# Dealing seven key tiles of two head pairs out around the sums and values of the preceding pairs in a fused attention and MLP kernel

## The chip, the cores and the metric

The kernel runs on one core of a Trainium2 chip. The metric is the device time of one execution in microseconds (us), the median over the runs shown. TensorE (PE) does the matrix products, ScalarE (ACT) the exponentials and activations, VectorE (DVE) reductions, scalings and copies, GpSimd (POOL) the squares and the loads that change type, and SyncE (SP) issues most other transfers. Each engine works through its own instructions strictly in the program's order.

## What is computed

Cosine attention over 8 batches of 12 heads, 448 positions of 64 numbers each, followed by a two-layer network with a leaky ReLU over all 3584 tokens.

```python
q_n = q / (np.linalg.norm(q, axis=-1, keepdims=True) + 1e-06)
k_n = k / (np.linalg.norm(k, axis=-1, keepdims=True) + 1e-06)
scores = np.matmul(q_n, k_n.transpose(0, 1, 3, 2)) / tau
scores = scores - np.max(scores, axis=-1, keepdims=True)
attn = np.exp(scores)
attn = attn / (np.sum(attn, axis=-1, keepdims=True) + 1e-09)
attn_out = np.matmul(attn, v)
...
x = np.ascontiguousarray(attn_out.transpose(0, 2, 1, 3)).reshape(B * S, H * D)
h = x @ w_in            # 768 -> 2048
g = np.maximum(0.01 * h, h)
return (g @ w_out).astype(np.float32)   # 2048 -> 768
```

## The kernel before

**Slots and pairs.** A slot `s` is two heads of one batch; there are 6 slots in a batch and 48 in all. Two consecutive slots, an even one and the odd one after it, make four heads. `j = s // 2 - 1` names the four heads whose sums and values are worked while the scores of slot `s` are made.

**Attention of a slot.** `load_qk(s)` (L94) issues four transfers on SP: queries, keys and two remainders of 64 rows. `squares(s)` (L130) squares them on POOL, `sums(s)` (L143) adds the squares up on DVE, `roots(s)` (L154) makes the norms with three small ACT instructions, and `normalise(s)` (L163) divides on DVE: one reciprocal and two multiplications into `qn`. `transposes(s)` (L194) turns `qn` into `qkT`. For slots under 10 this is seven PE transposes into PSUM and a DVE copy; from slot 10 on it is one transposing transfer on SP (`DMA_FROM = 10`).

**Key tiles.** The 448 keys of a head are three tiles of 128 and a rest of 64. `scores(s, kis)` (L210) issues for each tile `ki` the matmuls for both heads, then the exponentials on ACT. Tiles 0 to 2 use half of PE's rows for each head (64 rows by 128 columns), so both heads run side by side. Tile 3 holds the rests of both slots of a pair, so there are seven key tiles to two slots; it uses quarters of 64 by 64 and is made with the odd slot. The score pool `p_sc` has two buffers, so a key tile needs the exponential of the tile two before it.

**Sums and values.** `totals(j)` (L254) multiplies the exponentials by ones, `products(j, e)` (L264) by the even or odd columns of the values, both through `strip_products` (L242) in four column strips of 32 that run side by side: 16 matmuls each, 48 in all for one `j`. ACT makes the reciprocal sums (`rb`, L258 and L259), and `scale(j, e)` (L272) multiplies on DVE into `xT`.

**The network.** The tokens are cut into eight chunks of 384 or 512 columns in turn. `first(c, m)` (L287) makes one of 16 groups of 6 matmuls with an ACT activation into `hT`; `second(c, ts, half)` (L314) makes one of 6 or 8 groups of 16 matmuls with a DVE copy, and stores after the second half. All of these use the full 128 by 128 array. The list `work` (L343) gives each group a place, measured in slots: chunk `c` spreads over the six slots from `6(c+1)`. `feed(place)` (L358) issues all groups whose place has come. The PSUM pool `p_mm` has four buffers, shared by sums, values and groups.

**The order around the change.** The schedule is written out by hand. After an opening of six slots (L420), the main loop (L467) goes slot by slot. An even slot issues sums and values of the preceding four heads, key tiles 0 and 1, groups, the norms and transposes of slot `s + 2`, the loads of slot `s + 5`, key tile 2, groups. An odd slot does the same without sums and values, and ends with key tiles 2 and 3 together. On SP the transposing transfers, the loads and the stores stand in one queue in this order.

```python
for s in range(NPAIR, NSLOT + 1):
    j = s // 2 - 1 if s % 2 == 0 else None
    n = s + 2
```

Of the kernel before, what the change touches and what calls it, by code (L numbers as in the profile page):

```python
# [16 lines left out]
def kernel(  # L17
# [10 lines left out]
    nc = tc.nc  # L28
# [8 lines left out]
    NPAIR = H // 2  # L37
# [4 lines left out]
    HALF = D_model // 2  # L42
    DMA_FROM = 10
    WARM = 22
    assert REM == 64 and D == 64

    ctx.enter_context(tc.manual_schedule())
    cpool = ctx.enter_context(tc.tile_pool(name="consts", bufs=1))
    ldp = ctx.enter_context(tc.tile_pool(name="ld", bufs=4))
    vbp = ctx.enter_context(tc.tile_pool(name="vb", bufs=4))  # L50
    sqp = ctx.enter_context(tc.tile_pool(name="sq", bufs=2))
    smp = ctx.enter_context(tc.tile_pool(name="small", bufs=3))
    qnp = ctx.enter_context(tc.tile_pool(name="qn", bufs=3))
    qtp = ctx.enter_context(tc.tile_pool(name="qt", bufs=5))
# [58 lines left out]
    def load_v(j):  # L113
        if j >= B * NQ:
            return
        b, jj = divmod(j, NQ)
        vb[j] = vbp.tile([128, 4, 3, D], BF16, name="v_b")
        gp.dma_start(out=vb[j], in_=main(v, b, 4 * jj, 4))  # L118

    def load_v_rem(b):  # L120
        if b >= B:
            return
        r = v[b, :, MAIN:S].rearrange("(j g) p d -> g p j d", g=4)
        for g in range(4):
            lo = 64 * (g // 2)
            gp.dma_start(out=vrb[b % 2][lo : lo + 64, :, g], in_=r[g])  # L126
# [3 lines left out]
    def squares(s, engs=(gp, gp)):  # L130
        if s >= NSLOT:
            return
        tiles = []
        for x, eng, name in zip(raw[s], engs, ("sq0", "sq1")):
            sq = sqp.tile(list(x.shape), F32, name=name)
            if eng is nc.scalar:
                nc.scalar.activation(sq, x, func=AF.Square)  # L137
            else:
                eng.tensor_tensor(sq, x, x, op=ALU.mult)  # L139
            tiles.append(sq)  # L140
        sqs[s] = tiles
# [12 lines left out]
    def roots(s):  # L154
        if s >= NSLOT:
            return
        nc.scalar.activation(ss[s], ss[s], func=AF.Ln, bias=tiny)
        nc.scalar.activation(ss[s], ss[s], func=AF.Exp, scale=0.5)
        nc.scalar.activation(ss[s], ss[s], func=AF.Identity, bias=eps)  # L159
# [3 lines left out]
    def normalise(s):  # L163
        if s >= NSLOT:
            return
        r = smp.tile([128, 14], F32, name="r")
        nc.vector.reciprocal(r, ss[s])  # L167
        qn[s] = qnp.tile([128, 7, 2, D], BF16, name="qn")
        for x, lo, hi, r0 in ((raw[s][0], 0, 4, 0), (raw[s][1], 4, 7, 8)):
            nt = hi - lo  # L170
            nc.vector.tensor_tensor(  # L171
                qn[s][:, lo:hi],
                x.rearrange("p h t d -> p t h d"),
                r[:, r0 : r0 + 2 * nt].rearrange("p (h t) -> p t h", h=2)
                .unsqueeze(3).to_broadcast([128, nt, 2, D]),
                op=ALU.mult,
            )
# [32 lines left out]
    def scores(s, kis):  # L210

        if s >= NSLOT:
            return
        tiles = []
        for ki in kis:
            sc = scp.tile([128, 2, 512], F32, name="sc")
            tiles.append(sc)
            for i in range(2 if ki == 3 else 1):
                x = qkT[s - 1 + i] if ki == 3 else qkT[s]
                for a in range(2):  # L220
                    rows = slice(64 * a, 64 * a + 64)
                    out = sc[64 * i : 64 * i + 64] if ki == 3 else sc
                    c0, c1 = (448, 512) if ki == 3 else (512 + 128 * ki, 640 + 128 * ki)
                    nc.tensor.matmul(  # L224
                        out=out[:, a, :S], lhsT=x[rows, c0:c1], rhs=x[rows, 0:S],
                        start=True, stop=True,
                    )
        for ki, sc in zip(kis, tiles):
            if ki == 3:
                pr[s // 2] = prp.tile([128, 2, S], BF16, name="pr")  # L230
                dst = pr[s // 2]
            else:
                if s not in pe:
                    pe[s] = pep.tile([128, 3, 2, S], BF16, name="pe")
                dst = pe[s][:, ki]
            nc.scalar.activation(out=dst, in_=sc[:, :, :S], func=AF.Exp, scale=inv_tau)  # L236
# [17 lines left out]
    def totals(j):  # L254
        sm = mmp.tile([128, 512], F32, name="sm", tag="mm")
        strip_products(j, sm, lambda g, ki: ones, lambda g: ones_rem[:, g // 2])
        rb = rbp.tile([128, S], F32, name="rb")
        nc.scalar.activation(rb, sm[:, :S], func=AF.Ln)  # L258
        nc.scalar.activation(rb, rb, func=AF.Exp, scale=-1.0)  # L259
        rbs[j] = rb  # L260
# [3 lines left out]
    def products(j, e):  # L264
        b, jj = divmod(j, NQ)
        po = mmp.tile([128, 512], F32, name="po", tag="mm")
        pos[j, e] = po
        vm = vb[j].rearrange("p h t (d e) -> p h t e d", e=2)
        vr = vrb[b % 2].rearrange("p j g (d e) -> p j g e d", e=2)
        strip_products(j, po, lambda g, ki: vm[:, g, ki, e], lambda g: vr[:, jj, g, e])  # L270

    def scale(j, e):  # L272
        b, jj = divmod(j, NQ)
        m, half = divmod(b, 2)
        if m not in xT:
            xT[m] = xtp.tile([128, KT, 2 * S], BF16, name="xT")
        nc.vector.tensor_tensor(  # L277
            xT[m][:, 2 * jj + e, half * S : (half + 1) * S], pos.pop((j, e))[:, :S], rbs[j],
            op=ALU.mult,
        )  # L280
# [33 lines left out]
    def second(c, ts, half):  # L314
        c0, n = chunk_cols(c)
        po2 = mmp.tile([128, 512], F32, name="po2", tag="mm")
        for m in range(MT):
            nc.tensor.matmul(  # L318
                out=po2[:, :HALF],
                lhsT=hT[c][:, m, ts * 128 : (ts + 1) * 128],  # L320
                rhs=w_out_sb[:, m, half * HALF : (half + 1) * HALF],
                start=(m == 0), stop=(m == MT - 1),
            )
        if half == 0:
            osb[c, ts] = osp.tile([128, D_model], F32, name="osb")
        o = osb[c, ts]
        nc.vector.tensor_copy(out=o[:, half * HALF : (half + 1) * HALF], in_=po2[:, :HALF])  # L327
        last = c == B - 1 and ts == n // 128 - 1
        if half == 1 or last:
            h0 = half * HALF if last else 0  # L330
            x, end, row = c0 + ts * 128, c0 + (ts + 1) * 128, 0
            while x < end:
                dst, cnt = rows_of(c, x, end)
                nc.sync.dma_start(
                    out=dst[:, h0 : (half + 1) * HALF],
                    in_=o[row : row + cnt, h0 : (half + 1) * HALF],
                )
                x += cnt
                row += cnt
# [4 lines left out]
    for c in range(B):  # L344
        c0, n = chunk_cols(c)
        groups = [(6 * n, lambda c=c, m=m: first(c, m)) for m in range(MT)]
        order = [(ts, half) for half in range(2) for ts in range(n // 128)] if c == 0 else [
            (ts, half) for ts in range(n // 128) for half in range(2)
        ]
        groups += [  # L350
            (MT * HALF, lambda c=c, ts=ts, half=half: second(c, ts, half)) for ts, half in order
        ]
        total, done = sum(g[0] for g in groups), 0
        for cost, fn in groups:
            work.append((NPAIR * (c + 1) + NPAIR * (done + cost / 2) / total, fn))
            done += cost

    def feed(place):  # L358
        while work and work[0][0] <= place:
            work.pop(0)[1]()  # L360
# [103 lines left out]
            totals(j)  # L464
            products(j, 0)

    for s in range(NPAIR, NSLOT + 1):  # L467
        j = s // 2 - 1 if s % 2 == 0 else None
        n = s + 2
        squares(s + 3)  # L470
        if s % 2 == 1:
            load_v(s // 2 + 1)
        if s % NPAIR == 4:
            load_v_rem(s // NPAIR + 1)
        if s == NPAIR:
            load_w_out(1)
        if j is not None:
            totals(j)
            for e in range(2):
                products(j, e)  # L480
                scale(j, e)
        scores(s, (0, 1))
        if s == NPAIR:
            sums(s + 1)
            feed(s + 0.25)
            roots(s + 1)
            normalise(s + 1)
        else:
            sums(n)
        feed(s + 0.5)  # L490
        if s + 1 < DMA_FROM:
            transposes(s + 1)
        if s == NPAIR:
            sums(n)
        roots(n)
        normalise(n)
        if n >= DMA_FROM:
            transposes(n)
        load_qk(s + 5)
        scores(s, (2, 3) if s % 2 == 1 else (2,))  # L500
        feed(s + 1)
    feed(1e9)


# [33 lines left out]
```

## Time and profile before

| What | us |
|---|---|
| median of 3 runs (438.37 to 439.34) | 438.59 |
| the profiled execution's own time | 438.89 |
| its span, first to last instruction | 437.1 |
| busy in the span: ACT | 270.8 |
| busy in the span: DVE | 197.3 |
| busy in the span: POOL | 132.4 |
| PE, `second` groups (L318), 896 matmuls | 153.1 |
| PE, `first` groups (L293), 768 matmuls | 152.7 |
| PE, key tiles (L224), 384 matmuls | 53.2 |
| transposing transfers, issue to landing, median of 38 | 3.7 |
| query and key loads, issue to landing, median | 3.7 |

The span is the time between the first and the last instruction; the rest of the execution's own time, 1.8 us, lies around it. A group's busy time merges overlapping instructions, and matmuls are pipelined: a matmul of 384 columns is shown as 0.33 us, though the next one starts half that time later. So the pace of PE is read from start to start in the timeline. PE's clock stands at its full rate in all slices but the second one.

### The profile page before, as it was taken

Reading aid. Unit: us, or ns where it says so; the run is one execution under the profiler, and the core shown is the slowest. Engines: PE = TensorE matmul, PEld = TensorE weight load, DVE = VectorE, ACT = ScalarE, POOL = GpSimd, SP = SyncE. Lnnn points to the kernel's source line nnn. Section 1 sums busy time; section 2 is a strip of 40 time slices with the busy share of each in tenths; the row PEclk is TensorE's granted clock in tenths of the full one; section 3 lists DMA queues with packets and bytes.
Section 4 is the critical chain, followed back from the end, with each engine's and each line's share of the span. In section 5 each row is a group of like instructions: output and inputs, shape, how many; then the busy total and the mean of one; then the engine's idle time right before and its main releaser. Section 6 shows DMA issues by size and latency. Waiting matters only on the chain.

```text
span 437.1 us, 8497 instructions
## 1 busy us (share of the span) xinstructions
PE 425.5 (97%) x3319; PEld 206.7 (47%) x3319; DVE 197.3 (45%) x364; ACT 270.8 (62%) x495; POOL 132.4 (30%) x160
## 2 busy tenths in 40 slices
PE   8789899999999999999999999999999999999995
PEld 3234455544455554544455555544455554454563
DVE  5875744644454435633444545644425435220021
ACT  4898776477743886657744687658645598444300
POOL 4738542432352224442242312632242320000000
PEclk9699999999999999999999999999999999999999
DMA  8799999764456647744566575584476552110022
GB/s 168 159 234 237 210 208 166 148 155 104 85 110 153 129 117 140 151 122 92 103 138 154 100 142 95 111 206 81 72 148 153 138 104 40 57 73 1 0 73 72
DMA packets 104745, 54.11 MB, mean 124 GB/s; under 512 B 70785, under 2 KB 99713, under 8 KB 104705
## 3 DMA queue, kind: packets, MB, share of 16 engines
q1 hardware_dynamic: 79232, 41.54, 38.9%
q0 software_dynamic: 25056, 11.80, 21.8%
q8 instruction: 26, 0.43, 0.4%
q10 hardware_dynamic: 416, 0.23, 0.2%
q14 instruction: 15, 0.11, 0.1%
HBM read 45.61 MB, written 11.01 MB: 130 GB/s over the span
## 4 chain that ended last, share of the span: by engine, by line
PE 91%; DMA 3%; ACT 2%; DVE 2%; issue 0%; SPq 0%; DVEq 0%; ACTq 0%
PE po L318 34%; PE pm L293 33%; PE sc L224 10%; PE po L247 8%; PE sm L247 5%; DMA q_h<-in_q_dram 3%; ACT pe L236 1%; PE wm L387 1%; DMA q_h<-in_k_dram 1%; DVE qn L171 1%; PE tp L185 1%; DVE ss L150 0%; SPq L103 0%; ACT sq L137 0%; ACT ss L159 0%
## 5 line engine op out<-in xcount | busy, mean ns | idle before, releaser
L236 ACT ACTIVATE pe<-sc 128x896 bf16<-128x896 f32 x144 | 125.8, 913 | 52.3 <-PE sc L224 51.5
L318 PE MATMUL po<-w_out_sb,hT 128*128 128x384 bf16 x896 | 153.1, 326 | 0.0
L293 PE MATMUL pm<-xT,w_in_sb 128*128 128x384 bf16 (+1 forms) x768 | 152.7, 353 | 0.0
L318 PEld LDWEIGHTS <-hT 128*128 128x128 bf16 x896 | 84.2, 98 | 64.6 <-issue 12.0
L139 POOL TENSOR_TENSOR sq<-q_h 128x512 f32<-128x512 f32 x45 | 47.2, 1050 | 220.0 <-DMA q_h<-in_k_dram 183.1
L293 PEld LDWEIGHTS <-w_in_sb 128*128 128x128 bf16 x768 | 71.6, 98 | 74.7 <-issue 12.2
L299 ACT ACTIVATE hT<-pm 128x384 bf16<-128x384 f32 (+1 forms) x128 | 68.0, 545 | 34.8 <-PE pm L293 33.7
L327 DVE COPY osb<-po 128x384 f32<-128x384 f32 x56 | 31.2, 558 | 115.3 <-PE po L318 115.3
L224 PE MATMUL sc<-qkT 64*128 64x448 bf16 (+1 forms) x384 | 53.2, 367 | 4.2 <-ACT pe L236 3.2
L150 DVE TENSOR_REDUCE ss<-sq 128x8 f32<-128x512 f32 (+1 forms) x96 | 55.1, 610 | 1.2 <-ACT sq L137 0.7
L277 DVE TENSOR_TENSOR xT<-po,rb 128x448 bf16<-128x448 f32 x48 | 27.9, 620 | 42.8 <-ACT rb L259 42.8
L139 POOL TENSOR_TENSOR sq<-k_h 128x384 f32<-128x384 f32 x45 | 41.9, 930 | 0.0
L167 DVE RECIPROCAL r<-ss 128x14 f32<-128x14 f32 x48 | 11.3, 236 | 64.3 <-ACT ss L159 64.3
L171 DVE TENSOR_TENSOR qn<-q_h,r 128x512 bf16<-128x512 f32 x48 | 39.4, 820 | 1.6
L258 ACT ACTIVATE rb<-sm 128x448 f32<-128x448 f32 x24 | 13.0, 543 | 41.4 <-PE sm L247 41.4
L247 PE MATMUL po<-pe,v_b 128*32 128x448 bf16 x576 | 35.6, 353 | 0.0
L224 PEld LDWEIGHTS <-qkT 64*128 64x128 bf16 (+1 forms) x384 | 13.5, 96 | 45.4 <-issue 40.7
L171 DVE TENSOR_TENSOR qn<-k_h,r 128x384 bf16<-128x384 f32 x48 | 34.6, 721 | 0.0
L236 ACT ACTIVATE pr<-sc 128x896 bf16<-128x896 f32 x24 | 21.9, 913 | 0.6 <-PE sc L224 0.6
L247 PEld LDWEIGHTS <-v_b 128*32 128x32 bf16 x576 | 15.3, 97 | 11.9 <-issue 0.4
L126 POOL DMA_DIRECT2D v_rem<-in_v_dram x32 | 20.4, 642 | 0.0
L118 POOL DMA_DIRECT2D v_b<-in_v_dram x24 | 19.4, 807 | 0.0
(38 smaller groups left out, 163.4 us busy)
## 6 DMA issues: line engine op xcount, KB each, us to landing
q_h<-in_q_dram SPq DMA_DIRECT2D x48, 192.0 KB, 3.7
k_h<-in_k_dram SPq DMA_DIRECT2D x47, 192.0 KB, 3.7
out_dram<-osb SPq DMA_DIRECT2D x30, 192.0 KB, 2.7
v_b<-in_v_dram POOLq DMA_DIRECT2D x24, 192.0 KB, 4.2
out_dram<-osb SPq DMA_DIRECT2D x12, 384.0 KB, 3.1
w_in_sb<-in_moe_w_in_dram POOLq DMA_DIRECT2D x4, 768.0 KB, 10.5
w_out_sb<-in_moe_w_out_dram POOLq DMA_DIRECT2D x2, 1536.0 KB, 20.2
q_h<-in_q_dram SPq DMA_DIRECT2D x48, 32.0 KB, 3.7
```

The costliest lines, as they stand in the source:

```text
L126: gp.dma_start(out=vrb[b % 2][lo : lo + 64, :, g], in_=r[g])
L139: eng.tensor_tensor(sq, x, x, op=ALU.mult)
L150: nc.vector.tensor_reduce(o.rearrange("p (h t) -> p h t", h=2), sqs[s][i], axis=AX.X, op=ALU.add)
L171: nc.vector.tensor_tensor(qn[s][:, lo:hi], x.rearrange("p h t d -> p t h d"), r[:, r0 : r0 + 2 * nt].rearrange("p (h t) -> p t h", h=2) .u ...
L224: nc.tensor.matmul(out=out[:, a, :S], lhsT=x[rows, c0:c1], rhs=x[rows, 0:S], start=True, stop=True,)
L236: nc.scalar.activation(out=dst, in_=sc[:, :, :S], func=AF.Exp, scale=inv_tau)
L247: nc.tensor.matmul(out=x[32 * g : 32 * g + 32, :S], lhsT=weights(g, ki) if ki < 3 else rem(g), rhs=pe[s][:, ki, a, :] if ki < 3 else pr[j] ...
L277: nc.vector.tensor_tensor(xT[m][:, 2 * jj + e, half * S : (half + 1) * S], pos.pop((j, e))[:, :S], rbs[j], op=ALU.mult,)
L293: nc.tensor.matmul(out=pm[:, :n], lhsT=w_in_sb[:, kt, m * 128 : (m + 1) * 128], rhs=xT[c // 2][:, kt, c0 : c0 + n], start=(kt == 0), stop= ...
L299: nc.scalar.activation(out=hT[c][:, m, :n], in_=pm[:, :n], func=AF.Prelu, alpha=0.01)
L318: nc.tensor.matmul(out=po2[:, :HALF], lhsT=hT[c][:, m, ts * 128 : (ts + 1) * 128], rhs=w_out_sb[:, m, half * HALF : (half + 1) * HALF], st ...
L327: nc.vector.tensor_copy(out=o[:, half * HALF : (half + 1) * HALF], in_=po2[:, :HALF])
```

## The change

The main loop now goes in steps of two slots. Key tiles 0 and 1 of the even slot stand ahead of the sums and values of the preceding four heads, tile 2 of the even slot and tile 0 of the odd slot directly behind them; then come groups, tiles 1 and 2 of the odd slot, groups, tile 3, groups. Norms and transposes of the slots `s + 2` and `s + 3` follow the first and the second stretch of groups, with the loads of `s + 6` and `s + 7` behind each. The feeds are at a third and two thirds of the pair and at its end. Both `scale` calls now follow both `products` calls. Chunk 0 ends, and the others begin and end, 0.3 slots later. The squares have three buffers in place of two and are issued further ahead. The first of these pairs (slot 6) has an order of its own. In the last chunk's last group the copy is split between DVE and ACT, and the second of its two stores is issued from ACT.

```diff
+    LATE = 0.3
-    sqp = ctx.enter_context(tc.tile_pool(name="sq", bufs=2))
+    sqp = ctx.enter_context(tc.tile_pool(name="sq", bufs=3))
...
-        nc.vector.tensor_copy(out=o[:, half * HALF : (half + 1) * HALF], in_=po2[:, :HALF])
         last = c == B - 1 and ts == n // 128 - 1
+        cut = HALF // 2 if last and half == 1 else HALF
+        nc.vector.tensor_copy(out=o[:, half * HALF : half * HALF + cut], in_=po2[:, :cut])
+        if cut < HALF:
+            nc.scalar.copy(out=o[:, half * HALF + cut : (half + 1) * HALF], in_=po2[:, cut:HALF])
...
-                nc.sync.dma_start(
+                eng = nc.scalar if cut < HALF and row else nc.sync
+                eng.dma_start(
...
-            work.append((NPAIR * (c + 1) + NPAIR * (done + cost / 2) / total, fn))
+            start = NPAIR * (c + 1) + (LATE if c else 0)
+            end = NPAIR * (c + 2) + LATE
+            work.append((start + (end - start) * (done + cost / 2) / total, fn))
...
-    for s in range(NPAIR, NSLOT + 1):
-        j = s // 2 - 1 if s % 2 == 0 else None
-        n = s + 2
-        squares(s + 3)
-        if s % 2 == 1:
-            load_v(s // 2 + 1)
-        if s % NPAIR == 4:
-            load_v_rem(s // NPAIR + 1)
-        if s == NPAIR:
-            load_w_out(1)
-        if j is not None:
-            totals(j)
-            for e in range(2):
-                products(j, e)
-                scale(j, e)
-        scores(s, (0, 1))
-        if s == NPAIR:
-            sums(s + 1)
-            feed(s + 0.25)
-            roots(s + 1)
-            normalise(s + 1)
-        else:
-            sums(n)
-        feed(s + 0.5)
-        if s + 1 < DMA_FROM:
-            transposes(s + 1)
-        if s == NPAIR:
-            sums(n)
-        roots(n)
-        normalise(n)
-        if n >= DMA_FROM:
-            transposes(n)
-        load_qk(s + 5)
-        scores(s, (2, 3) if s % 2 == 1 else (2,))
-        feed(s + 1)
+    def attend(j):
+        totals(j)
+        for e in range(2):
+            products(j, e)
+        for e in range(2):
+            scale(j, e)
+
+    def norms(s):
+        roots(s)
+        normalise(s)
+        if s >= DMA_FROM:
+            transposes(s)
+
+    for s in range(NPAIR, NSLOT + 1, 2):
+        j, n = s // 2 - 1, s + 2
+        opening = s == NPAIR
+        squares(s + 3 if opening else n + 2)
+        if opening:
+            load_w_out(1)
+            attend(j)
+            scores(s, (0, 1))
+            sums(s + 1)
+            feed(s + 0.25)
+            norms(s + 1)
+            load_qk(s + 5)
+            feed(s + 0.8)
+            transposes(s + 1)
+            squares(n + 2)
+        else:
+            scores(s, (0, 1))
+            attend(j)
+        if s >= NSLOT:
+            break
+        load_v(s // 2 + 1)
+        scores(s, (2,))
+        scores(s + 1, (0,))
+        sums(n)
+        feed(s + (1.15 if opening else 0.67))
+        norms(n)
+        load_qk(n + 4)
+        squares(n + 3)
+        if (s + 2) % NPAIR == 0:
+            load_v_rem(s // NPAIR + 1)
+        scores(s + 1, (1, 2))
+        sums(n + 1)
+        feed(s + (1.6 if opening else 1.33))
+        norms(n + 1)
+        load_qk(n + 5)
+        if n < DMA_FROM:
+            transposes(n)
+        scores(s + 1, (3,))
+        feed(s + 2)
+        if n < DMA_FROM:
+            transposes(n + 1)
```

## The prediction

> **What bounds the kernel now.** I read the busy times first, then who made PE wait, then the timeline of PE.
>
> ```profile
> span 437.1 us, 8497 instructions
> PE 425.5 (97%) x3319; PEld 206.7 (47%) x3319; DVE 197.3 (45%) x364; ACT 270.8 (62%) x495; POOL 132.4 (30%) x160
> PE   8789899999999999999999999999999999999995
> ...
> PE sc L224 <- ACT pe L236: 3.2, 4, 1.6
> ...
> PE tp L185 <- DVE qn L171: 1.2, 2, 0.8
> ```
>
> PE is busy in nearly every slice, and what it waits for at all is a few microseconds, all before 50 us. So PE sets the end: time is won where PE's own stream gets shorter, and lost wherever the new order makes PE wait. The stretch before one attention shows how PE's stream is built (start, duration):
>
> ```profile
> 370.12 0.68 PE L224 MATMUL sc<-qkT 64*128 64x448 bf16 x6
> 370.72 2.77 PE L318 MATMUL po<-w_out_sb,hT 128*128 128x384 bf16 x16
> 373.43 0.75 PE L247 MATMUL sm<-pe,ones 128*32 128x448 bf16 x12
> 374.01 0.36 PE L247 MATMUL sm<-pr,ones_rem 128*32 128x448 bf16 x4
> ...
> 375.81 0.36 PE L224 MATMUL sc<-qkT 64*128 64x448 bf16 x2
> ```
>
> Three sets of four strips take 374.01 - 373.43 = 0.58, so 0.19 a set. Twelve sets would take 2.28, but the next key tile starts 2.38 after the first: 0.10 more. A matmul of 384 columns starts 0.163 after the one before (start to start inside a group), 16 of them 2.61, and the strips start 2.71 after the group: again 0.10 more. So each passage between the array's divisions (whole, 64 rows, 64 by 64, 32 columns) costs PE about 0.095 us; a step from a 64-row tile to a whole-array matmul is 0.28 against 0.19 between two tiles, the same again.
>
> **Fewer passages: -3.9.** Counted in the two programs' instruction order, PE changes division 248 times before and 207 times after, 10 against 8 in a pair of slots, with the same matmuls. 41 x 0.095 = 3.9 us, all on the path. Bounds: 41 x 0.08 = 3.3 and 41 x 0.10 = 4.1.
>
> **The tail: -0.7.**
>
> ```profile
> 432.63 0.56 DVE L327 COPY osb<-po 128x384 f32<-128x384 f32 x1 [2.04 <-PE po L318]
> 433.21 1.11 SPq L334 DMA_DIRECT2D out_dram<-osb  x2
> ```
>
> Nothing runs beside this. The second store is issued 0.52 behind the first on SP (1.11 for both, 0.59 for the second); on ACT's queue that goes. Half the columns on each engine save about 0.2 of 0.56, as a copy has a fixed part: the halves wait for each other, so -0.7 together, bounds -0.5 (the queue alone) and -0.9.
>
> **Edits at nothing.** The later chunks (0.3 slots) move groups that PE does anyway; the first groups of a chunk did not wait for `xT` before. Both `scale` calls behind both `products`: DVE idles there for `rb`. Sums and values between key tiles: the exponentials of tiles 0 and 1 (0.82 to 0.91 each, the reciprocal sums 1.1 behind them) now have 0.3 + 2.4 us of PE work as cover; tile 0 of the odd slot starts about 3.05 after tile 0 of the even one, and its score buffer is free at about 2.45, even with a last activation (0.6) in front on ACT. Cover gone, each 0.1 us late costs 0.1 in each of 21 pairs. Squares: a third buffer, and loads of two slots ahead, so POOL stays ahead.
>
> **What gets late: the transposing transfers.** From slot 10 on, `qkT` comes by a transfer on SP's queue. Before, it was issued one and a half slots ahead of its use. Now the odd slot's transfer is issued after the second stretch of groups, and its first use, tile 0 of that slot, comes ahead of the next stretch. What PE has in between is tile 3 to the groups (0.31), one stretch, two key tiles and a passage (0.49), the 48 strips with passages (2.38) and one tile (0.2). If the stretch is a single `second` group (2.70) that is 6.05 us. From the order, this is so at slots 10, 20, 22, 32 and 34; with `first` groups or two `second` groups it is 7.4 to 8.7.
>
> SP's queue decides the issue, since each transfer of the odd slot stands behind that of the even slot and its four loads:
>
> ```profile
> 165.97 1.26 SPq L200 DMA_TRANSPOSE qkT<-qn  x1
> 167.32 0.52 SPq L100 DMA_DIRECT2D q_h<-in_q_dram  x1
> 167.94 0.54 SPq L101 DMA_DIRECT2D k_h<-in_k_dram  x1
> 168.53 0.63 SPq L103 DMA_DIRECT2D q_h<-in_q_dram  x1
> 169.22 0.59 SPq L103 DMA_DIRECT2D q_h<-in_k_dram  x1
> 170.56 1.25 SPq L200 DMA_TRANSPOSE qkT<-qn  x1
> ...
> DMA to landing us min/median/max: 2.9/3.7/7.7
> ```
>
> Transfer and loads hold SP for 169.81 - 165.97 = 3.84. At slots 20 and 32 the even slot's transfer is issued 2.9 after tile 1 starts (activation 0.6, three norm instructions 0.9, reciprocal and two multiplications 1.4), so the odd slot's not before 6.8. Tile 3 starts at 0.49 + 18 x 0.163 + 0.1 = 3.5. That leaves 6.05 - 3.3 = 2.75 us to land: short by 0.15 at the least latency and by 0.95 at the median. Right behind loads in a quiet spell the latency was 2.9 (the transfer at 170.56), so I take 0.3, twice: 0.6.
>
> At slots 10, 22 and 34 groups are all `second`, DVE is through 2.07 after tile 1 (its copy ends the wait), and SP also has a store (0.54 and a gap, 0.65): the transfer is issued at 2.07 + 3.84 + 0.65 = 6.6, tile 3 starts at 0.49 + 2.70 = 3.2, so 6.05 - 3.4 = 2.65 remain. Short by 0.25 at the least latency, 1.05 at the median. In the trace the transfers issued within 0.3 us of a store landed after 4.3 to 4.7; I take 4.1, so 1.45, three times: 4.4 (bounds 0.75 and 6.2). PE's queue is in order, so groups, strips and all else stand behind the waiting tile, and nothing gives it back.
>
> At slot 8 the first transposing transfer meets the second half of `w_out` (landing 20.2 us after its issue at 46.5) as before, where it took the 7.7; it is now issued some 2 us later and needed at the same point. Bounds 0 and 2.0; the weights are nearly in by then, I take 0.4.
>
> A page bears on these waits. The Trainium skill, DMA: Bandwidth & Descriptors, in "Anatomy of one DMA", gives a transfer a fixed 2.0 us plus its bytes at 436 GB/s, fitted on GpSimd's path. As an estimate by that page the 224 KB of a transpose would land in 2.5 us, all five waits would be nothing, and the sum would be -3.7. The trace says otherwise, with 2.9 as the least of 38.
>
> **The opening pair: +0.5.** Before, PE waited about 2.2 us at slots 6 and 7:
>
> ```profile
> 44.18 0.81 PE L185 MATMUL tp<-id,qn 128*128 128x128 bf16 x7 [0.76 <-DVE qn L171]
> ...
> 48.48 0.37 PE L224 MATMUL sc<-qkT 64*128 64x448 bf16 x2 [0.85 <-ACT pe L236]
> ```
>
> A fourth `first` group (0.98) now covers most of the first, and the second falls. New ones: tile 0 of slot 7 right behind its transposes must wait for the DVE copy (0.62, less one tile: 0.5); transposes of slots 8 and 9 each come after only two groups (1.96), while norms need 3 us from the same point and DVE runs sums in between (about 0.7 each), and both copies queue behind the norms of slot 9 (0.3 to 0.8). About 2.7 against 2.2. Bounds -0.7 and +2.0.
>
> **The sum.** -3.9 - 0.7 + 0.6 + 4.4 + 0.4 + 0.5 = +1.3, on the profiled execution's 438.89: 440.2. The median of the runs is 0.3 lower than that execution, so 439.9. 0.2% is 0.9 us, about what a measurement of this kernel can tell from no change.
>
> **Rivals.** *Transfers land quickly (faster).* The place is the same five tiles; the mechanism is that a transfer right behind loads or a store starts as soon as its queue is free, so all land in 2.9 to 3.1. Then the waits are 2 x 0.25 + 3 x 0.35 = 1.5 in place of 5.0, and the time 439.9 - 3.5 = 436.4. For it: the 2.9 at 170.56; against it: the median of 3.7, and 4.3 and more behind stores. It decides from a latency below about 3.3 behind stores, where the sum falls under -0.9. *ACT's score buffers bind (slower still).* If ACT enters a pair 0.8 us later than I have it, tile 0 of the odd slot waits 0.2 in each of 21 pairs: +4, 443.9. For it: PE's only wait of this kind before was for ACT; against: ACT is 62% busy and catches up in every slot. *The passages are not saved.* If the array's change of division is not what costs the 0.095 but a first-tile latency that the same number of groups keeps paying, the gain is 0 to 1 and the time 443. Against: strips, tiles and groups all show the same 0.10.
>
> **Chances.** Forecast, waits of about 5 us and a time of 439.5 to 442.5: 0.44. Quick landings, 434.5 to 437.7: 0.29. In between, within 0.2% either way, where latencies average about 3.4: 0.19. The two slower rivals: 0.08. So faster 0.29, same 0.19, slower 0.52. All lows together give 434, all highs 447; for 8 in 10 I take 434.8 to 443.5, as the terms are not all off to one side.
>
> **What would show it.** Passages: key tiles and strips as 8 stretches in a pair, and a pair without waits 0.2 shorter. Waits: PE idle before `sc` with `qkT`'s transfer as releaser, at the second key tile behind the strips, in slots 12, 22, 24, 34 and 36 and nowhere else, largest behind a store. Tail: the two stores issued together and the end 4.0 rather than 4.5 after the last matmul. I am wrong if the transfers of the odd slots land in 3 us, if SP issues them sooner than the sum of its rows, or if PE waits for ACT inside the pairs.

## The result, and the profile after

The changed kernel takes 445.44 us (median of 6 runs, 444.84 to 446.8), the kernel before 438.62 beside it: a ratio of 1.0154, 95% interval 1.0137 to 1.0171. It is slower, as forecast, but by 6.8 us instead of 1.3, beyond the range of 434.8 to 443.5. One of the four runs of experiment 4 below, 452.38, was in a slower state of the chip, and that experiment's figures are of the other three.

The page of the changed kernel, the lines that answer to those shown of before:

```profile
span 443.5 us, 8509 instructions
PE 422.9 (95%) x3319; PEld 206.7 (47%) x3319; DVE 186.1 (42%) x364; ACT 270.0 (61%) x496; POOL 127.6 (29%) x160
...
PEclk9899998999999999999999999999999999999999
```

PE's busy time fell by 2.6 us (425.5 to 422.9) while the span grew by 6.4: PE has less to do and waits more. The second digit below 9 in the clock row, in the seventh slice, was not there before. The view of PE's waits names the releaser (us in total, times, longest):

```profile
PE sc L225 <- DMA qkT<-qn: 7.9, 5, 2.6
PE sc L225 <- ACT pe L237: 2.4, 3, 1.6
PE tp L186 <- DVE qn L172: 1.9, 4, 1.0
```

The first line is new: key tiles wait for the transposing transfers. The waits for ACT and DVE are within 1 us of those before. The largest of the new ones is not in an odd slot but at slot 10. Timeline of PE there (start, duration, ..., idle before and releaser):

```profile
65.66 5.37 PE L319 MATMUL po<-w_out_sb,hT 128*128 128x384 bf16 x32
73.66 0.93 PE L225 MATMUL sc<-qkT 64*128 64x448 bf16 x4 [2.63 <-DMA qkT<-qn]
74.51 1.31 PE L248 MATMUL sm<-pe,ones 128*32 128x448 bf16 x12
...
78.04 0.55 PE L225 MATMUL sc<-qkT 64*128 64x448 bf16 x4
```

The transfer that this tile waits for left SP at 65.72 and landed at 73.61. Before, it left at 63.68 and was first used at 73.38, behind the sums and values; now PE was ready for it at 71.03. The lines of before:

```profile
63.68 1.34 SPq L200 DMA_TRANSPOSE qkT<-qn  x1
...
73.38 0.55 PE L224 MATMUL sc<-qkT 64*128 64x448 bf16 x4
```

Behind the wait everything is slow at first: two key tiles take 0.93 where they took 0.55, twelve strips 1.31 where they took 0.75. The granted clock in two stretches of the same profile (PE, weight load, DVE, ACT and POOL busy, then the clock):

```profile
70.00:76.00 6.00, 3.37 (x31) 1.18 (x32) 0.56 (x1) 1.73 (x2) 0.25 (x1) 0.79 1.26 184
76.00:80.00 4.00, 4.00 (x50) 1.90 (x43) 2.30 (x4) 2.68 (x4) 2.85 (x4) 0.89 0.46 88
```

From 73.5 to 76.9 the clock stood at half. From the first key tile of slot 10 (73.66) to the third (78.04) PE needed 4.38; the same work took 2.87 in each of the 18 later pairs (in slot 36 from 290.37 to 293.24). So this one stretch of 3.4 us cost 1.51.

The odd slots look as foreseen. SP's queue from slot 36 to 37, and PE's timeline behind it:

```profile
286.22 1.26 SPq L201 DMA_TRANSPOSE qkT<-qn  x1
...
289.37 0.59 SPq L104 DMA_DIRECT2D q_h<-in_k_dram  x1
290.09 0.52 SPq L339 DMA_DIRECT2D out_dram<-osb  x1
290.73 1.31 SPq L201 DMA_TRANSPOSE qkT<-qn  x1
```

```profile
290.37 0.55 PE L225 MATMUL sc<-qkT 64*128 64x448 bf16 x4
...
293.24 0.36 PE L225 MATMUL sc<-qkT 64*128 64x448 bf16 x2
295.66 0.36 PE L225 MATMUL sc<-qkT 64*128 64x448 bf16 x2 [2.06 <-DMA qkT<-qn]
```

DVE had finished slot 37's `qn` at 289.61, but SP was still issuing four loads and a store; the transfer left 1.1 later, 4.51 behind that of slot 36, and landed at 295.61, 4.89 after its issue. Tile 2 of slot 36 starts at 293.24; tile 0 of slot 37, the very next one, had to wait. Taking each such tile's start to start less its usual spacing, the waits of the profiled execution are 2.70 (slot 10), 0.52 (13), 0.14 (23), 1.46 (25), 1.67 (35), 2.22 (37) and 0.24 (47): 8.95 in all.

The end of the changed kernel, with nothing beside it:

```profile
439.11 0.36 DVE L330 COPY osb<-po 128x192 f32<-128x192 f32 x1 [2.04 <-PE po L319]
439.50 0.32 ACT L332 COPY osb<-po 128x192 f32<-128x192 f32 x1 [20.59 <-DVE osb L330]
```

ACT's half of the copy starts when DVE's is through, and the view names DVE's copy as what released it. The two take 0.71 (439.11 to 439.82) where one took 0.56; from the start of the last matmul to the end of the span it is 4.73 against 4.86.

### The profile page after: what moved, and what is told of

It is laid out like the page before. It is cut to its first block, busy times and chain, and to the rows that moved or that the text cites. A ratio compares the mean times of both kernels' runs of the same rounds, so it can differ in the third digit from the quotient of the medians.

```text
span 443.5 us, 8509 instructions
## 1 busy us (share of the span) xinstructions
PE 422.9 (95%) x3319; PEld 206.7 (47%) x3319; DVE 186.1 (42%) x364; ACT 270.0 (61%) x496; POOL 127.6 (29%) x160
## 4 chain that ended last, share of the span: by engine, by line
PE 85%; DMA 10%; DVE 2%; ACT 2%; SPq 0%; issue 0%; ACTq 0%
PE pm L294 33%; PE po L319 32%; PE sc L225 9%; DMA qkT<-qn 6%; PE po L248 6%; PE sm L248 4%; DMA q_h<-in_q_dram 3%; DVE qn L172 1%; DMA q_h<-in_k_dram 1%; PE wm L394 1%; ACT pe L237 1%; PE tp L186 0%; DVE ss L151 0%; SPq L104 0%; DVE qkT L207 0%
## 5 line engine op out<-in xcount | busy, mean ns | idle before, releaser
L237 ACT ACTIVATE pe<-sc 128x896 bf16<-128x896 f32 x144 | 124.0, 912 | 68.0 <-PE sc L225 65.6
L294 PEld LDWEIGHTS <-w_in_sb 128*128 128x128 bf16 x768 | 72.7, 98 | 74.3 <-issue 9.8
L330 DVE COPY osb<-po 128x384 f32<-128x384 f32 (+1 forms) x56 | 31.0, 554 | 95.6 <-PE po L319 91.5
L225 PE MATMUL sc<-qkT 64*128 64x448 bf16 (+1 forms) x384 | 51.9, 365 | 12.3 <-DMA qkT<-qn 7.9
L140 POOL TENSOR_TENSOR sq<-k_h 128x384 f32<-128x384 f32 x45 | 37.4, 831 | 0.0
L172 DVE TENSOR_TENSOR qn<-q_h,r 128x512 bf16<-128x512 f32 x48 | 35.0, 730 | 2.2 <-DVE r L168 0.6
L225 PEld LDWEIGHTS <-qkT 64*128 64x128 bf16 (+1 forms) x384 | 12.3, 97 | 50.6 <-issue 35.8
L172 DVE TENSOR_TENSOR qn<-k_h,r 128x384 bf16<-128x384 f32 x48 | 27.1, 564 | 0.0
L158 ACT ACTIVATE ss<-ss,tiny 128x14 f32<-128x14 f32 x48 | 14.6, 304 | 9.3 <-DVE ss L151 9.3
```

Source lines behind the costliest of these rows:

```text
L172: nc.vector.tensor_tensor(qn[s][:, lo:hi], x.rearrange("p h t d -> p t h d"), r[:, r0 : r0 + 2 * nt].rearrange("p (h t) -> p t h", h=2) .u ...
L225: nc.tensor.matmul(out=out[:, a, :S], lhsT=x[rows, c0:c1], rhs=x[rows, 0:S], start=True, stop=True,)
L294: nc.tensor.matmul(out=pm[:, :n], lhsT=w_in_sb[:, kt, m * 128 : (m + 1) * 128], rhs=xT[c // 2][:, kt, c0 : c0 + n], start=(kt == 0), stop= ...
L330: nc.vector.tensor_copy(out=o[:, half * HALF : half * HALF + cut], in_=po2[:, :cut])
```

## The experiments

The kernels of one group ran beside their own runs of the kernel before (438.58 to 438.73). Each ratio is to the kernel before.

**1. The opening transfers on PE again.** Slots 10 and 11 get their transposes on PE.

```diff
-    DMA_FROM = 10
+    DMA_FROM = 12
```

> The transposes of slots 10 and 11 are made by PE instead of by transfers. Theory (the tile of slot 10 waits for a transfer that meets the second half of the output weights and two value loads, 2.7 us, and PE's clock then drops for some 4 us, 1.4 us more): the wait and the slow strips behind it go, 14 PE transposes and their two copies cost 0.9 to 1.5, so 442.3 to 443.1 against 445.4. Rival (the traffic at that point is late for everything, and the wait moves to the next tile): no change, 445.4.

Measured: 445.28 (443.76 to 449.63, 4 runs), ratio 1.0151 [1.0077, 1.0225]. The wait at slot 10 is gone, and nothing is won: PE waits 1.1 at the transposes of slot 11, 0.5 at slot 12 and 1.1 at slot 13, and the first key tile of slot 14 starts at 106.48 against 106.70. The profiled execution (449.63, the slowest of the four) has two stretches of 3.4 us at half clock, at 194 and 283 us, each behind a wait of PE of about 2 us for a transfer. The rival, that the wait moves on, holds.

**2. Loads behind both transfers.** On SP the four loads of the even slot go behind the odd slot's transfer.

```diff
         norms(n)
-        load_qk(n + 4)
+        if opening:
+            load_qk(n + 4)
...
         norms(n + 1)
+        if not opening:
+            load_qk(n + 4)
         load_qk(n + 5)
```

> The four loads that stood between the even and the odd slot's transposing transfer are issued behind the odd one. Theory (SP's queue makes the odd transfer late): it is issued 0.06 us behind its normalise instead of 0.4 to 1.1, and meets no loads on its way, so it lands in 2.9 to 3.1 us and the waits at slots 13, 23, 25, 35 and 37 (6.0 us) fall below 0.6; time 439.8 to 440.3. Rival (the transfers are slow whoever stands before them, as value loads share the engines): latencies of 4 to 5 stay at slots 25, 35 and 37, some 2.7 us of waits remain, and the time is 442. Slot 10's wait stays in both.

Measured: 441.77 (440.48 to 445.82, 10 runs), ratio 1.0063 [1.0029, 1.0097]. The odd transfers now leave 0.06 after `qn` is ready, and those of slots 13, 25 and 37 land in 2.9: their waits (4.2 together) are gone. But waits for transfers still sum to 6.2 on PE:

```profile
PE sc L225 <- DMA qkT<-qn: 6.2, 7, 3.0
```

Slot 10 keeps its own (3.0), slot 35 too (1.46, latency 4.34 though issued at once), slots 23 and 47 wait 0.38 each, and the even slots 24, 22 and 36 now wait (1.18, 0.27, 0.27). Their transfers had only 0.42, 0.70 and 1.22 to spare in the changed kernel. What used that up is DVE: its first multiplication into `qn` took 2.31, 1.63 and 1.25 for these three slots where it takes 0.69 when nothing is beside it, while POOL's squares ran (at slot 36 the transfer was 0.9 longer on its way too). The time lies between theory and rival, nearer the rival's 442: what stood ahead of the odd transfers on SP was the cause of the three odd waits, and without it other deadlines appear.

**3. Feeds at a half and the end.** The stretches of groups are at 0.5, 1.0 and 2.0 slots of the pair in place of 0.67, 1.33 and 2.0, so more groups stand between the odd slot's transfer and its use.

```diff
-        feed(s + (1.15 if opening else 0.67))
+        feed(s + (1.15 if opening else 0.5))
...
-        feed(s + (1.6 if opening else 1.33))
+        feed(s + (1.6 if opening else 1.0))
```

> The groups between the key tiles are dealt out at a quarter, a half and the end of a pair in place of thirds, so that half of them stand behind the odd slot's transfer. Theory (what is short is PE work between the transfer and its first use): 2.6 us more work there, no wait at slots 13 to 47, and slot 10's transfer is issued about 1 to 2 us earlier, so its wait falls to about 1 and PE's clock stays up; time 437.0 to 438.5, as the fewer passages are then seen. Rival (the fewer passages save nothing): 441 to 442 without waits.

Measured: 438.87 (437.39 to 440.71, 10 runs), ratio 0.9998 [0.9975, 1.0022]. This is just above the theory's range. Waits at slots 23 to 47 are gone; left are those at slot 10 (1.72) and 13 (1.25), and 1.8 more than in the changed kernel at PE's transposes in the opening:

```profile
PE tp L186 <- DVE qn L172: 3.7, 6, 0.9
...
PE sc L225 <- DMA qkT<-qn: 2.7, 2, 1.7
```

So all waits from slot 20 on come from where the stretches stand, not from the seven tiles being dealt out. What is left is the start. The transfer of slot 10 left no earlier than in the changed kernel (65.93), though the theory has it 1 to 2 us earlier; PE waits less for it because the opening kept PE 1.2 us longer.

**4. Work in place of the idle time at slot 10.** Twelve products whose result nothing uses go ahead of slot 10's key tiles in the changed kernel.

```diff
         else:
+            if s == DMA_FROM:
+                fill(12)
             scores(s, (0, 1))
```

> Twelve matmuls on constant data (12 x 0.216 = 2.6 us) are put on PE right ahead of the first key tile of slot 10, where it idles 2.6 us. Theory (the slow strips behind that gap are PE's clock, lowered by the idle time): the wait is filled, the strips run at 0.19 a set again, 1.0 to 1.4 us gained, 444.0 to 444.4. Rival (the strips are slow for another reason, such as the traffic): they stay at 0.36 a set, and the time is 445.4 or 0.1 more.

Measured: 445.18 (443.54 to 448.97, 3 runs), ratio 1.0149 [1.0068, 1.023]. The same two stretches as above, of this kernel:

```profile
70.00:76.00 6.00, 5.89 (x57) 2.75 (x59) 0.60 (x2) 1.44 (x2) 0.00 (x0) 1.00 1.20 156
76.00:80.00 4.00, 4.00 (x44) 2.00 (x36) 2.21 (x4) 3.39 (x7) 3.38 (x4) 1.00 0.50 115
```

The clock stays at 1.00 and the strips run at their usual pace (from the first key tile of slot 10 to that of slot 11 PE takes 3.07, in the changed kernel 4.58), so the slow strips were the clock's, brought on by the idle time. Yet the time is not better: PE waits 0.35 at slot 12 and 1.19 at 13 instead, and the first key tile of slot 14 starts at 106.69 against 106.70. Between slots 10 and 13 the transfers land when they land, and PE meets them at one place or another.

**5. Pairs from slot 10 on.** Slots 6 to 9 keep the order of before (with its feeds), the new order starts with the pair at slot 10 and has experiment 3's feeds; at slot 10 alone the loads stand behind both transfers. PE changes division 210 times.

```diff
-    for s in range(NPAIR, NSLOT + 1, 2):
-        j, n = s // 2 - 1, s + 2
-        opening = s == NPAIR
...
+    for s in range(NPAIR, DMA_FROM):
+        j = s // 2 - 1 if s % 2 == 0 else None
...
+    for s in range(DMA_FROM, NSLOT + 1, 2):
+        j, n = s // 2 - 1, s + 2
...
-        feed(s + (1.15 if opening else 0.67))
+        feed(s + 0.5)
...
-        feed(s + (1.6 if opening else 1.33))
+        feed(s + 1.0)
```

> Slots 6 to 9 keep the order of before; from slot 10 on the pairs of the change run, with groups dealt out at a quarter, a half and the end, and at slot 10 alone the loads behind the odd transfer. PE changes division 210 times, against 248 before and 207 in the change. Theory (the change loses by waits for transfers, and its fewer passages are real): no wait for a transfer above 0.5 us, and 438.6 - 38 x 0.095 = 435.0, within 434.6 to 435.8. Rival (passages cost PE nothing that it would not spend anyway): 438.0 to 438.6.

Measured: 437.14 (434.87 to 439.07, 10 runs), ratio 0.9961 [0.9941, 0.998]: faster than both kernels. The profiled execution is the fastest of them; there PE waits for a transfer once, 0.4 at slot 10. One other run lies in the expected range, and eight lie above it. Experiments 6 and 8, with the same order up to slot 12, show waits of 1.95 and 1.8 at slot 12. There the transfer itself was not slow (3.75 and 3.80), but it left 2.6 later, as DVE's multiplication took 2.99 and 2.79 where it took 0.69 in experiment 5. The lines of experiment 8 (DVE, and POOL's squares beside it):

```profile
78.57 2.79 DVE L172 TENSOR_TENSOR qn<-q_h,r 128x512 bf16<-128x512 f32 x1
78.97 1.05 POOL L140 TENSOR_TENSOR sq<-q_h 128x512 f32<-128x512 f32 x1
```

In experiment 5's profiled execution the load that these squares wait for landed at 79.85, in experiment 8's at 78.08, and so they began only when the multiplication was over. That is one source of the spread; as only one execution of each kernel was profiled, it is not shown that there is no other. From the first key tile of slot 14 to the last matmul this kernel takes 326.25, of which 2.59 are groups that before has already done by then; before takes 327.27 for the same. That is 3.6 less for the 34 passages between these points: 0.106 each.

**6. One key tile set apart.** Experiment 5, with tile 2 of the odd slot alone between groups: 243 passages, the same matmuls.

```diff
-        scores(s + 1, (1, 2))
+        scores(s + 1, (1,))
         sums(n + 1)
+        feed(s + 0.75)
+        scores(s + 1, (2,))
         feed(s + 1.0)
```

> The run before it, with key tile 2 of each odd slot moved into the middle of its stretch of groups, so that PE changes division 243 times in place of 210, all else the same. Theory (0.095 us for each passage): 33 x 0.095 = 3.1 us more than that run, 437.7 to 438.9. Rival (a passage costs nothing): the same time as that run.

Measured: 440.57 (439.13 to 442.43, 9 runs), ratio 1.0035 [1.001, 1.0059], 3.4 above experiment 5. From the sums of slot 14 to the last matmul it takes 329.05 against 325.77: 3.3 for the 31 passages that fall there, 0.106 each. The price of a passage, argued from three places in the prediction, is shown.

**7. Thirds in experiment 5.** The feeds of the change go back in.

```diff
-        feed(s + 0.5)
+        feed(s + 0.67)
...
-        feed(s + 1.0)
+        feed(s + 1.33)
```

> The first run of these four with the groups at thirds as in the change; slots 6 to 9 in the order of before. Theory (with thirds, the transfers of odd slots come too late wherever one group is all that stands behind them): waits at slots 23, 25, 35, 37 and 47 as in the change, 5.7 us together, and none at slots 10 to 13; 440.0 to 441.5, and 1.7 more where PE's clock drops. Rival (the waits follow from the late opening): no waits, 435.

Measured: 443.97 (442.73 to 444.39, 4 runs), ratio 1.0118 [1.01, 1.0136], 6.8 above experiment 5. The waits are back at 23, 25, 35, 37 and 47 (0.14, 1.18, 1.67, 1.95, 0.28), and so is a half-rate stretch, at 293.4, behind the idle time of slot 37. Together with experiment 3 this shows it both ways. It is above its range, since slots 10 and 12 wait here too (0.58, 1.8; DVE's multiplication for slot 12 took 2.18).

**8. The tail by rows.** Experiment 5, with the last copy split into rows 0 to 63 on DVE and 64 to 127 on ACT, into two SBUF tiles of their own.

```diff
+            for row, copy, eng in ((0, nc.vector.tensor_copy, nc.sync), (64, nc.scalar.copy, nc.scalar)):
+                oh = cpool.tile([128, HALF], F32, name=f"oh{row}")
+                copy(out=oh[row : row + 64], in_=po2[row : row + 64, :HALF])
```

> The first run of these four with the last group's copy split by rows into two tiles, 64 rows on DVE and 64 on ACT, each stored from its own queue. Theory (in the change ACT's half copy waited for DVE's because both write one tile): the two copies start together, last 0.56 each, and the end comes 4.5 to 4.6 us after the start of the last matmul, against 4.73 in the change and 4.86 before; 0.1 to 0.3 below the first run, too little for the times to tell apart. Rival (ACT is late for another reason): ACT's copy starts behind DVE's again and the end stays at 4.7 or more.

Measured: 437.31 (435.77 to 439.31, 10 runs), ratio 0.9971 [0.9958, 0.9985]. The end:

```profile
431.07 0.55 DVE L333 COPY oh<-po 64x384 f32<-64x384 f32 x1 [2.04 <-PE po L319]
...
431.65 0.47 ACT L333 COPY oh<-po 64x384 f32<-64x384 f32 x1 [20.79 <-DVE oh L333]
```

ACT again starts when DVE ends, with nothing shared but the PSUM tile that both read, and the end comes 4.77 after the start of the last matmul: the rival holds. So the shared output tile was not the reason. The view names DVE's copy as what released ACT's, so ACT waited for a signal from it; whether it would without the shared PSUM tile was not tried.

**9. Pairs from slot 12 on.** The order of before is kept up to slot 11; later chunks and feeds as in experiment 5. Other than there, the first new pair too has the loads ahead of the odd slot's transfer.

```diff
+    PAIRS_FROM = 12
-    for s in range(NPAIR, DMA_FROM):
+    for s in range(NPAIR, PAIRS_FROM):
...
-    for s in range(DMA_FROM, NSLOT + 1, 2):
+    for s in range(PAIRS_FROM, NSLOT + 1, 2):
```

> The feeds at a quarter, half and end again, with the old order now kept through slot 11, so that the two slots in which the second half of w_out and the first transposing transfers land have it too. Theory (the spread of the version with pairs from 10, 434.9 to 439.1, comes from waits at slots 10 to 12, where transfers are needed earlier after their issue in the order of pairs while w_out and the values still land): no wait of PE at slots 10 to 13 beyond 0.3, about two more passages than with pairs from 10 (+0.2), and the runs lie together: 434.3 to 435.5, median 434.8, spread under 2. Rival (wherever the pairs begin, the first of them waits): 1 to 2 us at slots 12 to 14 and a median of 436.5 to 438.

Measured: 437.31 (437.07 to 437.76, 6 runs), ratio 0.9967 [0.9954, 0.9979]. The runs lie together as the theory has it, but at the rival's height, and half of that is for the rival's reason. PE waits for ACT at slot 11, and at slot 13, in the first of the new pairs, for a transfer:

```profile
79.29 0.55 PE L226 MATMUL sc<-qkT 64*128 64x448 bf16 x4
80.66 0.37 PE L226 MATMUL sc<-qkT 64*128 64x448 bf16 x2 [0.82 <-ACT pe L238]
81.47 0.38 PE L226 MATMUL sc<-qkT 64*64 64x448 bf16 x4 [0.44 <-ACT pe L238]
...
88.73 0.10 PEld L226 LDWEIGHTS <-qkT 64*128 64x128 bf16 x2 [1.28 <-DMA qkT<-qn]
88.73 0.36 PE L226 MATMUL sc<-qkT 64*128 64x448 bf16 x2 [1.01 <-ACT pe L238]
```

All four key tiles of slot 11 stand together here, with no group between. That is the doing of the 0.3 slots by which chunk 0 ends later: one `second` group fewer falls into this place. Tile 0 of slot 13 waits another 1.01. The last line puts that down to ACT, but the line of the tile's weight load names the transfer, which landed at 88.69, and the score buffer that the tile needs was free at 86.63. The transfer had left 4.5 behind slot 12's, behind four loads and a store, and took 4.42.

**10. Without the later chunks.** Experiment 9 with the chunks where they were.

```diff
-    LATE = 0.3
+    LATE = 0.0
```

> The version with pairs from 12, with LATE 0: chunks begin and end 0.3 slots earlier, as in the kernel before. The prediction counted the 0.3 slots at nothing. Theory (the groups of a chunk's first stretch find xT ready either way, as they did before): within 0.5 of the version with 0.3. Rival (tile 2 of the even slot and tile 0 of the odd one, 0.49 of PE, are all that stands between the last values and the first group, and both multiplications into xT come behind both products): PE waits 0.3 to 0.8 for xT at the first group of a chunk, six times, 2 to 5 us slower.

Measured: 436.1 (435.61 to 436.86, 6 runs), ratio 0.994 [0.9925, 0.9955], 1.2 below experiment 9: outside the theory's 0.5, on the side that neither expected. At slot 11 a group stands between the tiles again, and no wait:

```profile
79.53 0.55 PE L226 MATMUL sc<-qkT 64*128 64x448 bf16 x4
80.01 2.77 PE L320 MATMUL po<-w_out_sb,hT 128*128 128x384 bf16 x16
```

Tile 0 of slot 13 still waits for its transfer, 0.47 in place of 1.01. The rival's wait for `xT` exists, but small: 0.24 at the first group of chunks 2, 4 and 6.

**11. The tail of before.** Experiment 9, with the last copy undivided on DVE and both stores on SP.

```diff
-        cut = HALF // 2 if last and half == 1 else HALF
+        cut = HALF
```

> The version with pairs from 12, with the last group's copy undivided on DVE and both stores on SP, as before. Theory (ACT's part of the copy waits for DVE's, so the two copies take about as long as the one, and only the second store's issue is spared): 0.1 to 0.3 slower than the version with pairs from 12, last matmul to end of span 4.86 against 4.73. Rival (the prediction's term): 0.7 slower. The tail's span will say it better than the medians.

Measured: 437.26 (436.82 to 437.58, 6 runs), ratio 0.9965 [0.9952, 0.9978]; from the start of the last matmul to the end 4.84, against 4.71 in experiment 9. The change's tail is worth 0.13 by the trace, which no median here can tell from nothing; the predicted 0.7 is excluded.

**12. Only the first chunk on time.** Experiment 9, with chunk 0 ending at slot 12 and the others 0.3 later.

```diff
-            end = NPAIR * (c + 2) + LATE
+            end = NPAIR * (c + 2) + (LATE if c else 0)
```

> The version with pairs from 12 (437.31), with chunk 0 ending at slot 12 as before, and only the others beginning and ending 0.3 slots later. Theory (LATE costs where chunk 0's `second` groups thin out: with it none stands between the key tiles of slot 11, which then wait 0.8 and 0.4 for ACT, and tile 1 of slot 13 waits 1.0; and LATE gains three first groups of 0.24 at chunks 2, 4 and 6): the waits at slot 11 are gone, those of 0.24 too, so 0.7 below LATE 0 at 436.1: 435.2 to 435.8, ratio about 0.993. Rival (the gap between the end of chunk 0 at 12 and the start of chunk 1 at 12.3 leaves slot 12 one group of 1.3 us where LATE 0 has three, and its tiles wait as those of slot 11 did): a wait of 0.8 or more at slots 12 and 13, and 436.1 to 437.3.

Measured: 436.04 (435.4 to 439.73, 12 runs), ratio 0.9947 [0.9924, 0.997]. The waits at slot 11 and the 0.24s are gone, but a wait of 0.8 for the transfer of slot 13 is left, as in experiment 10 (0.5). Nine runs lie within 435.4 and 436.2, three above 437; so keeping the old order up to slot 11 does not always hold the runs together. It can't be told from experiment 10; both beat the two kernels, by 2.5 us against the kernel before.

## Why the prediction failed in size

| term of the sum | predicted | in the profiled execution |
|---|---|---|
| slot 10's transfer (called slot 8's, first transfer) | +0.4 | +2.70 |
| the clock behind that wait | 0 | +1.51 |
| odd slots behind four loads (23, 35) | +0.6 | +1.81 |
| odd slots behind loads and a store (13, 25, 37) | +4.4 | +4.20 |
| slot 47 | 0 | +0.24 |
| tail | -0.7 | -0.13 |
| passages and opening together (the remainder) | -3.9 + 0.5 | -3.97 |
| sum | +1.3 | +6.36 (445.25 - 438.89) |

The right column is read from the trace, but for the remainder, which is what makes up the sum.

**The step that failed** is "it is now issued some 2 us later and needed at the same point". The first half is right: 65.72 against 63.68. The second is not. Before, key tile 0 of slot 10 came behind sums and values, at 73.38; now it stands in front of them, and PE got there at 71.03. By its own rows: issued 2.04 later, 0.18 longer under way (7.89 against 7.71), needed 2.35 sooner, less the 1.99 it had to spare, is 2.58 late; PE waited 2.63. "The weights are nearly in by then" failed with it: the second half of `w_out` landed at 69.97, 1.7 later than before, so it still lay beside the transfer. The bound of 2.0 is no more than the later issue alone. The prediction applied the earlier use to the odd slots and forgot it for the even ones. This wait and the clock behind it are 3.8 of the 5.1 us by which the sum fell short.

**A term that the prediction put at nothing** is the clock, which it did not mention. Experiment 4 shows that the idle time brought it on. A wait of about 2 us can bring it on, and then costs 1.5 (slot 10) to 1.7 more than its length (1.68 behind each of the three waits in experiments 1 and 7 that brought it on).

**Slots 20 and 32** (tile 0 of slots 23 and 35). The issue was sized well, 3.86 behind the even slot's against 3.84 predicted, and so was PE's work up to the tile (6.09 against 6.05, though the rows named there add up to 6.08). But the latencies were 2.93 and 4.47, where 0.3 of waiting on 2.75 of time means about 3.05 for both. Experiment 2 leaves slot 35's at 4.34 though SP had issued nothing for 2.2 us. The one thing beside it there, apart from the loads behind it, is a packet of 16 KB on the queue that the view of the DMA names `q8 instruction` (274.56, for 1.01 us); more on it in the last section.

**Slots 10, 22 and 34** (tile 0 of slots 13, 25 and 37). Right in place, cause and sum, 4.51 behind the even one's issue at slot 37 against 4.49. The single latencies were 3.19, 4.10 and 4.89 where 4.1 was taken; that their mean, 4.06, comes so near is in part luck. Experiment 2 shows the cause.

**The rival of quick landings** holds for most transfers: 25 of the changed kernel's 38 landed in 2.87 to 2.97. It fell at the tiles that decide, but for slot 23.

**Passages.** Right: 0.106 each in experiments 5 and 6 against 0.095, so 4.3 for the 41, a little beyond the bound of 4.1. The Trainium skill, TensorEngine Tiling (Array Packing), "Key Properties", says that changing the tiling mode drains TensorE. A cost at each such change agrees with it; that it is a drain, no run here shows.

**The opening** varies between executions. From the sums of slot 6 to PE's arrival at slot 10 it took 33.45 in the changed kernel, and 33.79 and 35.02 in experiments 2 and 3, which have the same order there; before, 33.54 with three passages more, which are 0.3. So it cost 0.2, 0.6 and 1.8, and the predicted +0.5 lies among them. (The 2.2 us that the prediction says PE waited there before are 1.61 by the lines that it shows.)

**Tail.** The halves of the copy do not run side by side, so what the queue saves is lost again (experiments 8 and 11).

**Edits at nothing.** In the changed kernel no wait shows for the squares (experiments 2, 6, 7 and 8 show that where they fall can cost 1 to 2 us), for both `scale` calls behind both products, or for ACT inside the pairs; the rival with ACT's score buffers fell. The later chunks were not free everywhere: with the old order up to slot 11 they cost 1.2 (experiments 9 and 10), and for the most part by chunk 0 alone (experiment 12). What they do in the changed kernel itself was not tried.

**What stays open.** Why the transfers of slots 10 to 13 take 4 to 8 us in some executions, beyond that the weights and the values land beside them; whether the packets of `q8 instruction` delay the transfers that they meet; and why the program has ACT's copy wait for DVE's.

## What to carry to other kernels

When work is dealt out anew, list for every transfer both its new issue and its new first use: here one transfer was issued 2 us later and used 2.4 sooner, and only the first was counted. Keep the new order out of the stretch where large loads still land, since taking one wait away there only uncovered the next (experiments 1 and 4). Elsewhere, moving the stretches of groups behind the late transfers took the waits away (experiment 3). Price a wait of 2 us on PE above its length, as it can cost the clock too.

## What the runs showed of the hardware

**The clock.** Idle stretches of PE of 2.63, 2.07, 1.84 and 1.79 us (changed kernel, experiment 1 twice, experiment 7) each brought one stretch of 3.41 us at half rate, which began between 0.2 before and 1.4 after their end; others of 2.98 (experiment 2), 2.06, 2.03, 2.01 (changed kernel, experiments 4 and 1) and 1.89 (experiment 6) brought none. So in this kernel a gap of 1.8 can be enough and one of 3.0 harmless. The Trainium skill, TensorE: Matmul & The Clock Gate, Part 1 ("What's actually happening") has a free-running window of 3413 ns; the lengths agree. Laid on a grid of such windows, read from where the clock changes in each trace, the four gaps that brought it on idle PE for 1.79 to 2.43 of one window, and the harmless ones of 2.0 to 3.0 for no more than 1.74 of any; but experiment 6's 1.89 lay whole in one window, so the grid alone does not decide it. Its table in "Why this matters for your kernels" advises against gaps over about 3 us; the runs show that shorter ones can cost the clock as well.

**The transfers.** Behind loads and a store on SP a transposing transfer took 3.2 to 4.9 in the changed kernel, and the first one, beside `w_out`, 7.7 to 8.2 in every run that has it at slot 10. In all traces, 186 transposing transfers had no earlier transfer and no load of POOL under way beside them: 150 of these landed in 2.87 to 2.99; the other 36, which had a packet of the queue `q8 instruction` or `q14 instruction` under way 0.8 to 2.9 us after their issue, took 2.91 to 4.69, all but two of them over 3.0. No run moved such a packet, so this is a coincidence seen 34 times and not a cause shown.

**DVE beside POOL.** Without POOL's squares beside it, DVE's first multiplication into `qn` took 0.69 to 0.82 in all 573 cases of the traces; the 99 that had some of the squares beside them took up to 2.99. Experiments 2, 6, 7 and 8 pay for that with late transfers.

**The copies.** A copy on ACT from a PSUM tile began 0.03 after a copy on DVE from other rows of the same tile ended, although they wrote to separate SBUF tiles. It waited for a signal of DVE's copy, so this is an order of the program, and no limit of the PSUM is shown by it.
